# Retention attention and two expert layers on one core: zero-filled half chunks, first-expert weight splits in half-size pieces, and an earlier load of the second weight quad

## The chip, the cores and the metric

The kernel runs on one core of one Trainium2 chip, as a single launch. The metric is device time in microseconds (us); lower is better. Five engines work side by side: TensorE (PE in the profile, with its weight loads as PEld), VectorE (DVE), ScalarE (ACT), GpSimd (POOL), and SyncE (SP), which here issues most of the DMA transfers.

## What is computed

The reference, cut to what matters (8 batches, 8 heads, 576 tokens per batch, head size 64; 4608 tokens of width 512; 8 experts):

```python
scores = scale * np.matmul(q, k.transpose(0, 1, 3, 2))
Dmat = np.where(rel >= 0, gamma[:, None, None] ** rel[None, :, :], 0.0)
ret = np.matmul(scores * Dmat[None], v)            # attention with decay, no softmax
x = ret as 4608 rows of 512
expert_idx = argmax(x @ w_gate);  gate_w = softmax probability of that expert
out[mask] = gate_w[mask, None] * (np.maximum(x[mask] @ w1[e], 0.0) @ w2[e])   # for each expert e
h = out @ w_in;  g = h * np.cos(h);  result = g @ w_out
```

## The kernel before, in words

There are three stages, one behind the other, and TensorE carries all three.

**Attention** walks 40 steps, 8 batches of 5 chunks of tokens (`CH`: four of 128 and a last one of 64, the half chunk). The loop over `i` is a software pipeline written out by hand: iteration `i` turns the keys of chunk `i+1` (`transposes`, L307), forms the masked products of queries and keys of chunk `i` (`scores`, PE L323, DVE L327), scales the keys of chunk `i+2` (`decay_k`, DVE L298), and finishes chunk `i-1`: `inter` (PE L348) adds what the running state of earlier chunks gives into the PSUM tile `xps`, `intra` (PE L358) adds the chunk's own part, DVE L361 takes `xps` away into `xt`, and PE L367 updates the state. `rows` (PE L379) turns chunk `i-2` back into rows and gate logits; ACT L381 and DVE L382 take them from PSUM. `xps` has one buffer, so the next `inter` waits until DVE L361 has read the last one. Each engine runs its instructions in the order of the program.

For the half chunk the order differs: its `inter` is called first thing in the iteration, ahead of `transposes`, and a small ACT copy named `between` (L554) reads `xps` so that `intra` starts behind it. The half chunk's `intra` multiplies over 64 rows.

Weights are used as a high and a low part in a reduced fp32 format: an ACT cast makes the high part, and a DVE subtraction the low one. For expert 0 this is done inside the attention loop by `unit_split` (ACT L202, DVE L203): eight splits of 128 x 1024, one every fourth iteration from `i` = 9 to 37. The DVE subtraction stands between `decay_k` and the `xt` multiplication of the same iteration. `unit_load` brings the weights in on SP's queue.

**The experts** (`layer1` L722, `layer2` L737) follow, 24 steps of work per expert. In the last expert `layer2` runs its four column blocks at steps 20 to 23; ACT L739 copies each result from PSUM into `yev`, of which there are two buffers, and SP L741 stores it into `ydT`. At step 16 `ws_load(0)` (L867) brings the first weight quad of the last stage into one of two `wquad` buffers. They lie where the last expert's first-layer weights were.

**The last stage** takes 72 quads. `product` (L1143) of quad `i` needs `units[2, i]`, that is `ws_load(i)`, and the operands `near` and `far` made by `enter` (ACT L642, DVE L643); `gate` and `down` (L1218) follow. Before the stage there is a branch for rare cases (`tc.If(late > 0)`, L1112) that is not taken here. SP gets past it only when its transfers have landed. Then come eight small matmuls into a spare PSUM bank (`warm(NWARM3)`, L212), the load of the token numbers (L1224), `ws_load(1)`, the three `far` operands, and the loop.

Of the kernel before, what the change touches and what calls it, by code (L numbers as in the profile page):

```python
# [22 lines left out]
P = 128  # L23
H = 8
# [17 lines left out]
NWARM3 = 8  # L42
# [76 lines left out]
def attn_moe_kernel(ctx, tc, qt, kv, wg, w1, w2, win, wout, ctab, out):  # L119
# [77 lines left out]
    def unit_split(key, g, pool):  # L197
        s = staged.pop((key, g))
        if g == 0:
            units[key] = pool.tile([P, 2, 4, 512], F32R, tag=unit_tag(pool, key), name="wunit")  # L200
        u = units[key]
        nc.scalar.copy(out=u[:, 0, 2 * g:2 * g + 2], in_=s)  # L202
        nc.vector.tensor_sub(out=u[:, 1, 2 * g:2 * g + 2], in0=s, in1=u[:, 0, 2 * g:2 * g + 2])  # L203

# [10 lines left out]
    with ExitStack() as actx:  # L215
# [53 lines left out]

        steps = [(b, c) for b in range(B) for c in range(NCH)]  # L270
# [10 lines left out]
        def load_kv(i):  # L281
            b, c = steps[i]
            o, n = CH[c]
            t = ap3.tile([P, 2, H, D], F32, tag="ldkv", name="ldkv", bufs=6)
            nc.sync.dma_start(out=t[:n].rearrange("p s h d -> p s (h d)"), in_=kv[b * SEQ + o:b * SEQ + o + n])
            st[i]["k"], st[i]["v"] = t[:, 0], t[:, 1]
# [26 lines left out]
        def scores(i):  # L313
            b, c = steps[i]
            o, n = CH[c]
            s = st[i]
            pT = ap2.tile([P, H, P], F32, tag="pT", name="pT")
            scs = [ps1.tile([P, 4, P], F32, tag="sc", name="sc", bufs=3) for g in range(2)]

            for j in range(4):  # L320
                for g, r in ((0, 0), (1, D), (0, D), (1, 0)):
                    if r < n:
                        mm(out=scs[g][r:r + D, j, :n], lhsT=s["kpT"][D * g:D * g + D, j, r:r + D],  # L323
                           rhs=s["qT"][D * g:D * g + D, j, :n], start=(j == 0), stop=True, skip_group_check=True)
            m = mask[:n, :n].unsqueeze(1).to_broadcast([n, 4, n])
            for g in range(2):
                nc.vector.tensor_mul(out=pT[:n, g::2, :n], in0=scs[g][:n, :, :n], in1=m)  # L327
            s["pT"] = pT
# [22 lines left out]
        def intra(i):  # L351
# [4 lines left out]
            for h in range(H):  # L356
                k, r = place_of(h)
                mm(out=xp[r:r + D, k, :n], lhsT=s["v"][:n, h, :], rhs=s["pT"][:n, h, :n],  # L358
# [187 lines left out]
        wq = [(key, g) for key in w_units(0) for g in range(2)]  # L546
        waiting = []
        between = ap1.tile([P, 2, 2, 1], F32, name="between")
        for i in range(NS + 5):

            short = 1 <= i <= NS and CH[steps[i - 1][1]][1] <= D
            if short:
                inter(i - 1)
                nc.scalar.copy(out=between, in_=st[i - 1]["xp"].rearrange("p (a j) t -> p j a t", a=2)[:, 0:2, :, 0:1])  # L554
            if i + 1 < NS:
                transposes(i + 1)
            if i < NS:
                scores(i)
            if i + 2 < NS:
                decay_k(i + 2)  # L560
            if i >= 9 and (i - 9) % 4 == 0 and (i - 9) // 4 < len(wq):
                unit_split(*wq[(i - 9) // 4], upA)
            if i == 0:
                setup()
            if 1 <= i <= NS:
                if not short:
                    inter(i - 1)
# [8 lines left out]
            if 0 <= i - 2 < NS:  # L576
                rows(i - 2)
            to_spread, placed[:] = placed[:], []
# [11 lines left out]
            if i >= 6 and (i - 6) % 4 == 0 and (i - 6) // 4 < len(wq):  # L590
                unit_load(ap3, *wq[(i - 6) // 4])

        assert not tabled and not routed and not waiting and not placed
        assert not tabled and not routed
# [65 lines left out]
    with ExitStack() as mctx:  # L660
# [285 lines left out]
        for e in range(E):  # L946
# [9 lines left out]
            for i, (hf, l, k) in enumerate(work):  # L956
# [38 lines left out]
                if e + 1 == E and i == 16:  # L995
                    ws_load(0)
# [122 lines left out]
    warm(NWARM3, psA.tile([P, 512], F32, tag="h", name="hps", bufs=4), ident)  # L1119


# [110 lines left out]
    ws_load(1)  # L1232
# [81 lines left out]
```

## Time and profile before

| | us |
|---|---|
| median of 3 runs | 1423.28 (1420.9 to 1426.21) |
| the profiled execution | 1419.5 |
| its span in the profile | 1417.7 |
| PE busy | 1381.1 (97% of the span) |
| DVE busy | 964.5 (68%) |
| ACT busy | 705.6 (50%) |
| POOL busy | 223.0 (16%) |

The span is one execution from the first to the last instruction that the profiler saw; the execution's own time is 1.8 us longer. A busy share is an average over the three stages. The rows further down show single stretches: for each group, what the engine did, for how long, and in square brackets how long it had been idle before and on what it had waited.

### The profile page before, as it was taken

Reading aid. Unit: us, or ns where it says so; the run is one execution under the profiler, and the core shown is the slowest. Engines: PE = TensorE matmul, PEld = TensorE weight load, DVE = VectorE, ACT = ScalarE, POOL = GpSimd, SP = SyncE. Lnnn points to the kernel's source line nnn. Section 1 sums busy time; section 2 is a strip of 40 time slices with the busy share of each in tenths; the row PEclk is TensorE's granted clock in tenths of the full one; section 3 lists DMA queues with packets and bytes.
Section 4 is the critical chain, followed back from the end, with each engine's and each line's share of the span. In section 5 each row is a group of like instructions: output and inputs, shape, how many; then the busy total and the mean of one; then the engine's idle time right before and its main releaser. Section 6 shows DMA issues by size and latency. Waiting matters only on the chain.

```text
span 1417.7 us, 28604 instructions
## 1 busy us (share of the span) xinstructions
PE 1381.1 (97%) x11427; PEld 1284.0 (91%) x11427; DVE 964.5 (68%) x1953; ACT 705.6 (50%) x1405; POOL 223.0 (16%) x334
## 2 busy tenths in 40 slices
PE   8999979999999999998999999999999999999998
PEld 6888859999999999997999999899999999999997
DVE  5878768675888676854667666676667667676654
ACT  2444414444554544533556555565555655555554
POOL 3444441223221323200000010100101010010101
PEclk9999979999999999999999999999999999999999
DMA  7777725566776766795464564645646455555541
GB/s 240 231 243 232 234 73 173 183 220 211 242 251 201 224 206 229 251 384 203 178 230 172 191 232 162 249 169 197 226 157 241 182 213 196 196 199 197 187 175 64
DMA packets 81306, 292.23 MB, mean 206 GB/s; under 512 B 13476, under 2 KB 22128, under 8 KB 70928
## 3 DMA queue, kind: packets, MB, share of 16 engines
q1 hardware_dynamic: 68240, 248.33, 50.9%
q0 software_dynamic: 12928, 42.02, 8.6%
q8 instruction: 91, 1.49, 0.4%
q14 instruction: 47, 0.39, 0.1%
HBM read 238.85 MB, written 51.47 MB: 205 GB/s over the span
## 4 chain that ended last, share of the span: by engine, by line
PE 42%; issue 11%; POOL 1%; DMA 1%; ACT 0%; POOLq 0%
PE acc L1218 22%; PE hps L1143 20%; POOL out_dram L1200 1%; DMA wquad<-ws 1%; PE hps L212 0%; POOLq L1310 0%; POOL spare L156 0%; ACT ka L1173 0%; ACT orow L1198 0%; ACT gh L1184 0%; PE acc L1229 0%; POOLq L1200 0%
## 5 line engine op out<-in xcount | busy, mean ns | idle before, releaser
L1218 PE MATMUL acc<-wunit,gh 128*128 128x512 f32 x1152 | 358.3, 392 | 0.1
L1143 PEld LDWEIGHTS hps<-far,wquad 128*128 128x128 f32 x1920 | 244.6, 191 | 7.3
L1143 PE MATMUL hps<-far,wquad 128*128 128x256 f32 x1920 | 249.3, 283 | 0.0
L1218 PEld LDWEIGHTS acc<-wunit,gh 128*128 128x128 f32 x1152 | 207.3, 189 | 36.2 <-ACT gh L1184 0.3
L1218 PE MATMUL acc<-wunit,gl 128*128 128x512 f32 x576 | 224.4, 390 | 0.0
L722 PE MATMUL hps<-xT,wunit 128*128 128x256 f32 (+6 forms) x1536 | 208.6, 296 | 0.9 <-ACT xT L707 0.7
L737 PE MATMUL hps<-hh,wunit 128*128 128x256 f32 (+6 forms) x1024 | 207.7, 298 | 0.0
L722 PEld LDWEIGHTS hps<-xT,wunit 128*128 128x128 f32 x1536 | 206.4, 188 | 1.4 <-ACT xT L707 0.9
L737 PEld LDWEIGHTS hps<-hh,wunit 128*128 128x128 f32 x1024 | 164.3, 188 | 0.1
L1200 POOL DMA_INDIRECT out_dram<-orow,perm x36 | 35.0, 972 | 757.2 <-DVE orow L1196 751.4
L1143 PE MATMUL hps<-near,wquad 128*128 128x256 f32 x1104 | 147.5, 286 | 4.4 <-DMA wquad<-ws 4.4
L737 PE MATMUL hps<-hl,wunit 128*128 128x256 f32 (+6 forms) x512 | 151.3, 296 | 0.0
L1143 PEld LDWEIGHTS hps<-near,wquad 128*128 128x128 f32 x1104 | 142.9, 194 | 8.2 <-issue 4.6
L1218 PEld LDWEIGHTS acc<-wunit,gl 128*128 128x128 f32 x576 | 108.2, 188 | 24.7 <-DVE gl L1186 1.1
L1180 DVE SCALAR_TENSOR_TENSOR sa<-sa,quad 128x512 f32<-128x512 f32 x144 | 99.1, 688 | 42.8 <-ACT sa L1178 42.8
L1184 ACT CAST gh<-sa 128x512 fp32r<-128x512 f32 x144 | 89.6, 622 | 74.8 <-DVE sa L1180 74.8
L1154 DVE TENSOR_TENSOR part<-hps,part 128x256 f32<-128x256 f32 x72 | 30.6, 425 | 132.1 <-PE hps L1143 126.7
L1186 DVE TENSOR_TENSOR gl<-sa,gh 128x512 fp32r<-128x512 f32 x144 | 98.9, 687 | 20.4 <-ACT gh L1184 14.9
L1175 DVE SCALAR_TENSOR_TENSOR sa<-quad,ka 128x512 f32<-128x512 f32 x144 | 99.0, 687 | 12.2 <-ACT ka L1173 12.2
L1153 ACT COPY part<-hps 128x256 f32<-128x256 f32 x72 | 26.8, 372 | 144.2 <-PE hps L1143 137.9
L737 PEld LDWEIGHTS hps<-hl,wunit 128*128 128x128 f32 x512 | 96.5, 188 | 0.0
L1177 ACT ACTIVATE sa<-sa 128x512 f32<-128x512 f32 x144 | 91.3, 634 | 8.8 <-DVE sa L1175 8.8
(195 smaller groups left out, 1897.1 us busy)
## 6 DMA issues: line engine op xcount, KB each, us to landing
wquad<-ws SPq DMA_DIRECT2D x72, 1792.0 KB, 7.4
wst<-in_moe_w_dram SPq DMA_DIRECT2D x64, 512.0 KB, 5.1
ldkv<-in_kv_dram SPq DMA_DIRECT2D x32, 512.0 KB, 4.7
ws<-cvo POOLq DMA_DIRECT2D x56, 256.0 KB, 3.8
ldq<-in_qt_dram SPq DMA_DIRECT2D x32, 256.0 KB, 4.3
xd<-xs SPq DMA_DIRECT2D x32, 256.0 KB, 2.5
cvw<-in_moe_w_in_dram SPq DMA_DIRECT2D x16, 512.0 KB, 4.8
cvw<-in_moe_w_out_dram SPq DMA_DIRECT2D x16, 512.0 KB
```

Source lines behind the costliest of these rows:

```text
L722: mm(out=ph[:, :n], lhsT=u[:, a, kc, f0:f0 + P], rhs=t[:, bq, kc, :n], start=(idx == 0), stop=(idx == 11))
L737: mm(out=py[:, :n], lhsT=u[:, w], rhs=t[:, :n], start=(fc == 0 and g == 0), stop=(fc == 7 and g == 2))
L1143: mm(out=o, lhsT=u[:, s, kc, a], rhs=x[:, bq, kc], start=(s in (0, 1, 2) and idx == 0), stop=(idx == 5), skip_group_check=True)
L1153: nc.scalar.copy(out=p1, in_=x[:, :HT])
L1154: nc.vector.tensor_add(out=u2, in0=y[:, :HT], in1=p1)
L1175: nc.vector.scalar_tensor_tensor(out=sa, in0=x, scalar=INV2PI, in1=ka, op0=ALU.mult, op1=ALU.subtract)
L1177: nc.scalar.activation(out=sa, in_=sa, func=AF.Sin, scale=math.pi)
L1180: nc.vector.scalar_tensor_tensor(out=sa, in0=sa, scalar=-1.0, in1=x, op0=ALU.add, op1=ALU.mult)
L1184: nc.scalar.copy(out=gh, in_=sa)
L1186: nc.vector.tensor_sub(out=gl, in0=sa, in1=gh)
L1200: ins = nc.gpsimd.indirect_dma_start(out=out[:, :], out_offset=bass.IndirectOffsetOnAxis(ap=perm[:, k:k + 1], axis=0), in_=o, in_offset=None)
L1218: mm(out=acc2[T][c], lhsT=pair[n][:, fh, c % 2 * P:(c % 2 + 1) * P], rhs=u[:, w, fc % 4], start=(q == 0 and fh == 0 and n == 0 and w == 0) ...
```

## The change

- The half chunk's `inter` goes back to its usual place behind `scores`, and the copy `between` is gone. The half chunk has tiles of its own: `halfkv` (two, by the batch's parity) and `halfpT` (one). Rows 64 to 127 of the value half and of `halfpT` are zeroed once by POOL, and `intra` multiplies over all 128 rows.
- Expert 0's weights are split in 16 pieces of 128 x 512 in place of 8 of 128 x 1024: one piece in each batch's fifth iteration and two in the next one, from `i` = 9 to 34. The ACT casts stand behind `transposes`, the DVE subtractions behind `rows`. The loads move to iterations 6, 7, 11, 15, 16, 21, 25 and 26.
- `ws_load(1)` is issued at step 20 of the last expert in place of behind the branch.
- The eight matmuls of `NWARM3` are gone.

```diff
+        halfkv = [ap1.tile([P, 2, H, D], F32, name=f"halfkv{i}") for i in range(2)]
+        halfpT = ap1.tile([P, H, D], F32, name="halfpT")
+        for t in [t.rearrange("p s h d -> p s (h d)")[D:, 1] for t in halfkv] + [halfpT[D:]]:
+            nc.gpsimd.memset(t, 0.0)
...
-            t = ap3.tile([P, 2, H, D], F32, tag="ldkv", name="ldkv", bufs=6)
+            t = ap3.tile([P, 2, H, D], F32, tag="ldkv", name="ldkv", bufs=6) if n == P else halfkv[b % 2]
...
-            pT = ap2.tile([P, H, P], F32, tag="pT", name="pT")
+            pT = ap2.tile([P, H, P], F32, tag="pT", name="pT") if n == P else halfpT
...
-                mm(out=xp[r:r + D, k, :n], lhsT=s["v"][:n, h, :], rhs=s["pT"][:n, h, :n],
+                mm(out=xp[r:r + D, k, :n], lhsT=s["v"][:, h, :], rhs=s["pT"][:, h, :n],
...
-        wq = [(key, g) for key in w_units(0) for g in range(2)]
+        wq = dict(zip((6, 7, 11, 15, 16, 21, 25, 26), [(key, g) for key in w_units(0) for g in range(2)]))
+        pieces = [(key, f) for key in w_units(0) for f in range(4)]
...
-            short = 1 <= i <= NS and CH[steps[i - 1][1]][1] <= D
-            if short:
-                inter(i - 1)
-                nc.scalar.copy(out=between, in_=st[i - 1]["xp"].rearrange("p (a j) t -> p j a t", a=2)[:, 0:2, :, 0:1])
             if i + 1 < NS:
                 transposes(i + 1)
+            now = [pieces.pop(0) for _ in range({NCH - 1: 1, 0: 2}.get(i % NCH, 0) if i > NCH else 0) if pieces]
+            for key, f in now:
+                if f == 0:
+                    units[key] = upA.tile([P, 2, 4, 512], F32R, tag="unit", name="wunit")
+                nc.scalar.copy(out=units[key][:, 0, f], in_=staged[key, f // 2][:, f % 2])
             if i < NS:
                 scores(i)
             if i + 2 < NS:
                 decay_k(i + 2)
-            if i >= 9 and (i - 9) % 4 == 0 and (i - 9) // 4 < len(wq):
-                unit_split(*wq[(i - 9) // 4], upA)
...
-                if not short:
-                    inter(i - 1)
+                inter(i - 1)
                 intra(i - 1)
...
                 rows(i - 2)
+            for key, f in now:
+                nc.vector.tensor_sub(out=units[key][:, 1, f], in0=staged[key, f // 2][:, f % 2], in1=units[key][:, 0, f])
...
-            if i >= 6 and (i - 6) % 4 == 0 and (i - 6) // 4 < len(wq):
-                unit_load(ap3, *wq[(i - 6) // 4])
+            if i in wq:
+                unit_load(ap3, *wq[i])
...
-                if e + 1 == E and i == 16:
-                    ws_load(0)
+                if e + 1 == E and i in (16, 20):
+                    ws_load((i - 16) // 4)
...
-    warm(NWARM3, psA.tile([P, 512], F32, tag="h", name="hps", bufs=4), ident)
...
-    ws_load(1)
```

How the order of instructions changes. First VectorE in iterations 9 and 10, the end of the second batch (`pT` are the masks, `kp` the scaled keys, `xt` the multiplication that frees `xps`, `lgt` the logits), before:

```order
L327 TENSOR_TENSOR pT<-sc,ca 64x4x64 x2
L298 TENSOR_TENSOR kp<-ldkv,ca 128x512
L203 TENSOR_TENSOR wunit<-wst,wunit 128x1024
L361 TENSOR_TENSOR xt_126<-xps,gx 128x512
L382 TENSOR_REDUCE lgt_132<-rw 128x8 x2
L327 TENSOR_TENSOR pT<-sc,ca 128x4x128 x2
L298 TENSOR_TENSOR kp<-ldkv,ca 128x512
L361 TENSOR_TENSOR xt_122<-xps,gx 128x4x64
```

and with the change:

```order
L323 TENSOR_TENSOR halfpT<-sc,ca 64x4x64 x2
L294 TENSOR_TENSOR kp<-ldkv,ca 128x512
L357 TENSOR_TENSOR xt_126<-xps,gx 128x512
L378 TENSOR_REDUCE lgt_132<-rw 128x8 x2
L572 TENSOR_TENSOR wunit<-wst,wunit 128x512
L323 TENSOR_TENSOR pT<-sc,ca 128x4x128 x2
L294 TENSOR_TENSOR kp<-ldkv,ca 128x512
L357 TENSOR_TENSOR xt_122<-xps,gx 128x4x64
L502 TENSOR_TENSOR tab<-tab,lg 128x120
L378 TENSOR_REDUCE lgt_132<-rw 128x8 x2
L572 TENSOR_TENSOR wunit<-wst,wunit 128x512 x2
```

The subtraction has moved from ahead of `xt` to behind the logits, and has become three smaller ones over the two iterations.

TensorE at the end of a batch, where a half chunk is finished, before:

```order
L379 MATMUL rw<-wgi,xt_124 128x136 x4
L348 MATMUL xps<-ldq,sbd_128 64x64 x8
L307 MATMUL tp<-ct,kp 128x128 x4
L323 MATMUL sc<-ldq,kpT 64x128 x16
L358 MATMUL xps<-pT,ldkv 64x64 x8
```

and with the change:

```order
L375 MATMUL rw<-wgi,xt_124 128x136 x4
L303 MATMUL tp<-ct,kp 128x128 x4
L319 MATMUL sc<-ldq,kpT 64x128 x16
L344 MATMUL xps<-ldq,sbd_128 64x64 x8
L354 MATMUL xps<-halfpT,halfkv_135 64x64 x8
```

`inter`, which writes `xps`, now has `transposes` and `scores` ahead of it.

SyncE at the end of the last expert, before (`ydT` are the stores of the four column blocks):

```order
L867 DMA wquad<-ws_74 128x3584
L1008 REGISTER_ALU
L1008 DMA idc<-sidT 5x128
L741 ISA
L741 DMA ydT<-yev 128x232
L741 ISA
L741 DMA ydT<-yev 128x232
```

and with the change:

```order
L861 DMA wquad<-ws_74 128x3584
L1002 REGISTER_ALU
L1002 DMA idc<-sidT 5x128
L735 ISA
L735 DMA ydT<-yev 128x232
L861 DMA wquad<-ws_74 128x3584
L735 ISA
L735 DMA ydT<-yev 128x232
```

The second quad's load now stands between the first and the second of the four stores.

## Rows read from the trace of the kernel before

**Rows 1.** Stretches: busy us (instructions) per engine, PEclk granted clock, DMA share, GB/s.

```profile
0.00:216.00 216.00, 192.78 (x3455) 169.49 (x3456) 155.27 (x455) 75.91 (x180) 88.49 (x140) 0.95 0.65 207
...
643.50:666.00 22.50, 17.09 (x109) 15.59 (x109) 10.21 (x20) 8.73 (x17) 0.00 (x0) 0.85 0.68 249
```

**Rows 2.** Timeline, DVE in iteration 9: start, us, what.

```profile
50.46 1.21 DVE L203 TENSOR_TENSOR wunit<-wst,wunit 128x1024 fp32r<-128x1024 f32 x1
51.60 0.67 DVE L361 TENSOR_TENSOR xt<-xps,gx 128x512 f32<-128x512 f32 x1
```

**Rows 3.** Timeline, PE at two batch ends, the first with a split, the second without.

```profile
52.41 0.46 PE L348 MATMUL xps<-ldq,sbd 64*64 64x64 f32 x16 [0.97 <-DVE lgt L382]
...
96.01 0.63 PE L367 MATMUL S<-ldkv,kp 128*64 128x64 f32 x16
...
97.70 0.46 PE L348 MATMUL xps<-ldq,sbd 64*64 64x64 f32 x16
...
99.60 0.64 PE L358 MATMUL xps<-pT,ldkv 64*64 64x64 f32 x16
```

**Rows 4.** Timeline, PE: the same place in four batches, five iterations apart each.

```profile
30.15 0.66 PE L307 MATMUL tp<-ct,kp 128*128 128x128 f32 x4
...
121.08 0.66 PE L307 MATMUL tp<-ct,kp 128*128 128x128 f32 x4
...
144.81 0.65 PE L307 MATMUL tp<-ct,kp 128*128 128x128 f32 x4
...
167.67 0.66 PE L307 MATMUL tp<-ct,kp 128*128 128x128 f32 x4
```

**Rows 5.** Half-size subtractions in the expert stage: count, min/median/max ns, first to last start.

```profile
L854 DVE TENSOR_TENSOR wunit<-wst,wunit x112: 673/686/744, 223.7 to 602.2; 128x512 fp32r<-128x512 f32 x112
```

**Rows 6.** Timeline, POOL at the start.

```profile
10.26 1.78 POOL L253 TENSOR_SCALAR gx<-gx,ca 128x128 f32<-128x128 f32 x3 [7.73 <-DMA ca<-in_consts_dram]
```

**Rows 7.** Timeline, PE from the last expert into the last stage.

```profile
643.29 0.27 PE L737 MATMUL hps<-hl,wunit 128*128 128x232 f32 x1
644.15 0.60 PE L212 MATMUL hps<-ct 128*128 128x256 bf16 x4 [0.59 <-ACTq L1112]
...
645.51 3.12 PE L1143 MATMUL hps<-near,wquad 128*128 128x256 f32 x24
648.47 2.31 PE L1143 MATMUL hps<-far,wquad 128*128 128x256 f32 x18
655.19 5.21 PE L1143 MATMUL hps<-near,wquad 128*128 128x256 f32 x24 [4.42 <-DMA wquad<-ws]
```

**Rows 8.** Timeline, ACT over the same stretch.

```profile
641.24 0.35 ACT L739 COPY yev<-hps 128x232 f32<-128x232 f32 x1 [2.61 <-DMA ydT<-yev]
643.64 0.35 ACT L739 COPY yev<-hps 128x232 f32<-128x232 f32 x1 [2.05 <-PE hps L737]
646.38 0.62 ACT L642 CAST far<-yfirst 128x512 fp32r<-128x512 f32 x1 [2.39 <-SPq L1112]
```

**Rows 9.** Timeline, SP's queue: the first quad's load, the second of four stores.

```profile
627.56 0.32 SPq L867 DMA_DIRECT2D wquad<-ws  x1
...
638.66 0.33 SPq L741 DMA_DIRECT2D ydT<-yev  x1
```

**Rows 10.** The chain that ended last, at the second quad: start, us, what.

```profile
647.22 7.83 DMA wquad<-ws
655.19 7.36 PE hps L1143 x42
```

**Rows 11.** DMA issues of one line: count, KB each, median us from issue to landing.

```profile
wquad<-ws SPq DMA_DIRECT2D x72, 1792.0 KB, 7.4
```

**Rows 12.** Stretches, columns as in rows 1: three in which TensorE stood.

```profile
6.50:9.00 2.50, 0.02 (x1) 0.05 (x1) 0.69 (x1) 0.59 (x1) 0.00 (x0) 1.00 1.01 350
650.80:653.00 2.20, 0.00 (x0) 0.00 (x0) 1.88 (x5) 0.63 (x1) 0.00 (x0) 1.00 1.05 440
653.00:655.20 2.20, 0.01 (x1) 0.04 (x1) 0.00 (x0) 0.00 (x0) 0.00 (x0) 0.53 0.91 358
```

More of the change, by code (lines that the diff above doesn't have):

```diff
@@ L41 @@
 NWARM2 = 11
-NWARM3 = 8
 INV2PI = 1.0 / (2.0 * math.pi)
@@ L195, in unit_load @@
         staged[key, g] = s
[L197 to L203, printed above, removed]
     def w_units(e):
@@ L545, in attn_moe_kernel @@
         decay_k(1)
-        wq = [(key, g) for key in w_units(0) for g in range(2)]
+        wq = dict(zip((6, 7, 11, 15, 16, 21, 25, 26), [(key, g) for key in w_units(0) for g in range(2)]))
+        pieces = [(key, f) for key in w_units(0) for f in range(4)]
         waiting = []
-        between = ap1.tile([P, 2, 2, 1], F32, name="between")
         for i in range(NS + 5):
-            short = 1 <= i <= NS and CH[steps[i - 1][1]][1] <= D
-            if short:
-                inter(i - 1)
-                nc.scalar.copy(out=between, in_=st[i - 1]["xp"].rearrange("p (a j) t -> p j a t", a=2)[:, 0:2, :, 0:1])
             if i + 1 < NS:
                 transposes(i + 1)
+            now = [pieces.pop(0) for _ in range({NCH - 1: 1, 0: 2}.get(i % NCH, 0) if i > NCH else 0) if pieces]
[3 more added lines that the diff above has]
+                nc.scalar.copy(out=units[key][:, 0, f], in_=staged[key, f // 2][:, f % 2])
             if i < NS:
@@ L589, in attn_moe_kernel @@
                 loads(i + 4)
-            if i >= 6 and (i - 6) % 4 == 0 and (i - 6) // 4 < len(wq):
-                unit_load(ap3, *wq[(i - 6) // 4])
-        assert not tabled and not routed and not waiting and not placed
-        assert not tabled and not routed
+            if i in wq:
+                unit_load(ap3, *wq[i])
+        assert not tabled and not routed and not waiting and not placed and not pieces
         rp = ps1.tile([P, 8, P], F32, tag="x", name="xps").rearrange("p a t -> p (a t)")
```

## The prediction, made before the changed kernel was run

> **What bounds the kernel now.** I first read busy time by stretch, to see where TensorE is not the limit, then the timeline and the waits inside those stretches. In the attention stage TensorE is busy 192.78 of 216 us; in the 22.5 us around the start of the last stage it is busy 17.09, and its clock is granted at 0.85 on average [rows 1]. Everywhere else it hardly stands, so the change can only pay in these two stretches, both of which it touches.
>
> In attention the thing to see is a queue on VectorE. In iteration 9 the subtraction of the weight split (1.21 us from 50.46) stands ahead of the `xt` multiplication, which starts at 51.60 [rows 2]. TensorE's early `inter` writes the single-buffered `xps` and needs `xt` done: it stands 0.97 us and starts at 52.41. The wait is labelled with the logits, the next instruction on VectorE. At a batch end without a split the same `inter` starts at 97.70 with no wait [rows 3]. So the early place of `inter` costs nothing alone; with a split it does.
>
> Is that one case or all? Batches differ in how many splits they hold. From 30.15 to 121.08 there are four batches with one split each (iterations 9, 13, 17, 21), 90.93 us; the batch from 144.81 to 167.67, 22.86 us, has one (33); the one from 121.08 to 144.81, 23.73 us, has two (25, 29) [rows 4]. One-split batches average (90.93 + 22.86) / 5 = 22.76 us, so a second split costs 23.73 - 22.76 = **0.97 us**, the wait seen directly. I charge it to all eight, wherever they stand: 8 x 0.97 = 7.8 us.
>
> At the handover the experts end at 643.56 (643.29 + 0.27). The warm-up matmuls begin at 644.15, and the first quad's products run from 645.51 to 650.78 (648.47 + 2.31). Then TensorE stands 4.42 us for the second quad's weights [rows 7]. Their load was issued at 647.22 and took 7.83 us; the products behind it took 7.36 us, against 650.78 - 645.51 = 5.27 us for the first quad [rows 10]. That is the clock: it was granted whole until 653.00, in a stand that began at 650.78, and averaged 0.53 from there to 655.20 [rows 12], about the lower level (1.2 of 2.4 GHz).
>
> **The change, part by part.** *Splits.* Removed: eight waits, 7.8 us. Added: 16 subtractions of 0.686 us [rows 5], 11.0 us of VectorE against 8 x 1.21 = 9.7 us, so 1.3 us more work, but behind the logits. The next work there is the masks, which need the next `scores`. From `inter` to `intra` at the clean batch end, with `transposes` and `scores` between, TensorE takes 99.60 - 97.70 = 1.9 us [rows 3]; the largest group of pieces is 2 x 0.686 = 1.37 us, so it fits. If that cover fails, the masks come late and then `rows`, whose PSUM buffers the masks free. Bounds: nothing, or a wait in proportion to a piece's length, 0.97 x 0.686 / 1.21 = 0.55 us, 16 times, 8.8 us. I take 0.05 us each, 0.8 us, near the lower end, since the pieces stand behind the work that TensorE waits for. The casts stand behind the key copy and delay only ACT copies that wait for matmuls two microseconds later. Loads come at least two iterations ahead of their first piece. Net gain in attention: 7.8 - 0.8 = **7.0 us**.
>
> *Half chunk.* `inter` moves behind two groups of matmuls, and `xt` has that time more. The copy `between` goes. The 64-row `intra` takes 0.64 us for 16 passes; a 128-row group of equal count and width (the state update) takes 0.63 us [rows 3]. So the zeros cost no TensorE time: 0. POOL's three fills fall into the 7.73 us in which it stands for its constants [rows 6]: 0; without that cover they delay decay tables that are needed only in iteration 2 and later.
>
> *Second quad.* Its load moves from 647.22 to just behind the first of the last four stores, at about 636.4 (the second store is issued at 638.66 [rows 9]). It needs 7.4 to 7.8 us [rows 10, 11], so it lands near 644, six microseconds ahead of its use. Gone: the 4.42 us wait, and with it 7.36 - 5.27 = 2.1 us of slow clock.
>
> But the load is queued ahead of three stores, and they free `yev`. A store behind a large load waits: the copy at 641.24 had stood 2.61 us for the first store, which had the first quad's load of 627.56 ahead of it in the queue; the next copy, at 643.64, waited only for TensorE [rows 8, 9]. If the second store lands with the load ahead of it, at about 644.0, the fourth `yev` copy, which needs that buffer, starts there in place of 643.64 and ends at 644.4. The Trainium skill, page DMA: Bandwidth & Descriptors, section Queues, rings and completion order, says that on each DMA engine the descriptors of one ring are consumed in ring order; by that rule the store cannot pass the load, and the trace's late copy agrees. My two ends for this: no delay, and the fourth copy late by the 2.61 us that the third one stood, at 646.25. I take 0.4 us, since the load's landing is the nearer row.
>
> *No warm-up.* TensorE was released at 644.15, 0.16 us behind the end of the last copy (643.64 + 0.35) [rows 7, 8]. With the copy ending at 644.4 the first quad starts at 644.5, not 645.51: 1.0 us gained. Its `far` operands come when SP is past the branch, which was 2.39 us behind the copy's end [rows 8]: 646.8, and 0.62 us of cast and a subtraction of about 0.69 us [rows 5] make the first one whole at 648.1. The first 24 matmuls take 648.47 - 645.51 = 2.96 us, to 647.5, so I put 0.4 us of new wait there. Gain left: 0.6 us. The stand grows from 0.59 us to about 1.0 us. At 6.50 to 9.00 TensorE stood as good as all of 2.50 us and the clock stayed at 1.00; at 653 it fell after some 2.3 us of standing [rows 12]. So I expect it to hold. The Trainium skill, page TensorE: Matmul & The Clock Gate, section Why this matters for your kernels, speaks against this edit: it warns of idle gaps between bursts of matmuls, which put the array back on its lower clock. By that rule the first quad would be slow; rows 12 show both outcomes.
>
> *Third quad.* Its load still starts when the first quad's products end, now about 650.2. Its use comes one product and one half `down` later: 5.27 + 2.9, at 658.4; 7.4 us [rows 11] land it at 657.9. Half a microsecond of slack is thin, and the gate chain of the first quad no longer hides behind a slow product: I charge 0.5 us for both.
>
> Handover: 4.4 + 2.1 + 0.6 - 0.5 = **6.6 us**.
>
> **Sum.** 7.0 + 6.6 = 13.6 us off the profiled execution's 1419.5 (span 1417.7 and 1.8 around it): 1405.9. That execution lies 3.8 us under the median of the runs, 1423.28; on the median's scale the forecast is 1423.3 - 13.6 = **1409.7 us**. The experts and the steady last stage run at TensorE's pace and only shift.
>
> **The rivals.**
> 1. *The pieces still show.* VectorE, busy 155 of 216 us in attention [rows 1], falls behind at batch ends and half of the old wait stays. For: three subtractions in two neighbouring iterations, with the routing behind them. Against: their place. Attention gives 3.5 in place of 7.0: 1413.2.
> 2. *The clock falls at the handover.* With the warm-up gone and the stores late, TensorE's stand becomes one like that from 650.78. The first quad is slow by 2.1 us, and starts up to 646.25 - 644.0 = 2.2 us later: 1409.7 + 4.3 = 1414.0.
> 3. *The wait moves to the third quad.* Its load finds two loads of encoded rows, 512 KB each, ahead of it in SP's queue: 1,048,576 bytes at the 440 GB/s of a full stretch [rows 12] are 2.4 us, so it lands at 650.2 + 7.4 + 2.4 = 660.0, 1.6 us late, and if the clock falls, 2.1 us more: 1411.3 to 1413.4.
> 4. *Slower than before.* Small pieces cost as much each as a whole split did, because what counts is a late instruction on VectorE and not its length: 16 x 0.97 = 15.5 in place of 7.8, 7.7 us lost, more than the handover's 6.6: 1424.4. It decides from (7.8 + 6.6) / 16 = 0.90 us for each piece. Against: the pieces come behind `xt`, not ahead of it.
> 5. *The early load does nothing*, because SP, held by stores that wait for `yev`, issues it late. SP issues it ahead of the second store, whose issue is seen at 638.66 [rows 9], so it would have to slip nine microseconds: 1409.7 + 6.5 = 1416.2.
>
> **How the numbers follow.** Forecast 0.60; rivals in order 0.13, 0.12, 0.10, 0.02, 0.03. A difference of 0.5% is 7.1 us, about what a measurement of this kernel can tell from no change, so the edge is 1416.2. The forecast and the first three rivals lie beyond it, 0.95, unless two of the rivals meet, for which I take 0.07; with rival 5's 0.03 that is the same: faster 0.88, same 0.10, slower 0.02. The low end is no cost for pieces, gate chain and stores (0.8 + 0.5 + 0.4 + 0.4 = 2.1 us less) and 2.4 us for the spread of the runs (1420.9 against the median): 1405. The high end takes in two of the first three rivals together: 1417.
>
> **What would show it.** Right: no TensorE wait at batch ends; batches of about 21.8 us (22.76 - 0.97); no wait for `wquad` at the second quad; a clock at 1.00 from 644 to 666; third quad's products near 658 less what attention gained. Wrong: a wait on masks or logits in iterations 10, 15, 20; a clock under 1.00 in the first quad's products; a `yev` copy that waits for its store until past 645 (on the old time axis); a wait for the third quad.

## The result, and the profile after

The changed kernel took **1408.1 us** (median of 4 runs, 1405.9 to 1411.57). The kernel before, on the same chip, took 1422.09 us (median of 4, 1418.86 to 1426.21). The ratio is **0.9915, interval 0.9895 to 0.9934**: faster by 0.85%, 12.1 us (the two medians lie 14.0 us apart; the ratio with its interval is what is used here). The forecast of 13.6 us off is a ratio of 0.9904, inside the interval; 1409.7 us stood against 1408.1. The sum was right, but by luck: attention gave more than its term, the handover less, and the two errors cancelled.

To see that, cut both profiled executions at five marks that every kernel here has: the first `transposes` of iteration 5 (30.15 in [rows 4]), the last `transposes` of attention, the first matmul of expert 0, the end of the experts, and the first product of the third quad. The numbers are taken on TensorE's timeline: each mark is the start of its instruction, the end of the experts is the end of their last matmul, and "rest" ends with the span.

| stretch, us | before | after | difference |
|---|---|---|---|
| start, to iteration 5 | 30.15 | 33.13 | +2.98 |
| attention, steady | 150.32 | 142.27 | -8.05 |
| last iterations, to expert 0 | 33.83 | 32.52 | -1.31 |
| experts | 429.26 | 431.30 | +2.04 |
| handover, to the third quad | 21.99 | 18.91 | -3.08 |
| rest | 752.15 | 751.67 | -0.48 |
| span | 1417.70 | 1409.80 | -7.90 |

The first mark has one flaw. Where the half chunk's `inter` comes early, its 0.39 us lie ahead of the mark (29.76 to 30.15 before); in the other kernels it lies behind. With equal work on both sides, the start differs by 3.37 us and steady attention by -8.44.

The difference of this pair of executions, 7.9 us, is smaller than that of the medians, and the two rows with a plus say why. This execution (1411.57 us) is the longest of the four, and its slow stretches are clock. Stretches of the changed kernel; columns as in [rows 1]:

```profile
8.00:10.00 2.00, 0.57 (x4) 0.58 (x4) 0.69 (x1) 0.00 (x0) 0.00 (x0) 0.90 1.04 338
10.00:12.00 2.00, 2.00 (x34) 1.59 (x32) 0.00 (x0) 0.58 (x1) 1.18 (x2) 0.50 1.02 391
...
18.00:20.00 2.00, 2.00 (x30) 1.93 (x27) 1.92 (x4) 0.00 (x0) 2.00 (x4) 0.54 0.09 33
...
212.00:214.00 2.00, 2.00 (x11) 2.00 (x11) 0.37 (x3) 0.26 (x1) 0.00 (x0) 0.50 0.64 194
```

The granted clock is 0.50, the lower of its two levels, from 10 to past 18 us and again in the first six microseconds of expert 0. At 6.50 to 9.00 before it was 1.00 in the same place [rows 12]. That is no part of the change: in the ten kernels that follow, the start took from 29.32 to 34.16 us, 29.80 and 29.82 with all of the changed attention stage, and the experts 428.25 to 429.48. So these two rows are left out of the account, and what the change did is read from the other four: -8.05, -1.31, -3.08 and -0.48, together **-12.9 us** (-13.3 with the 0.39), near the 12.1 of the runs.

**Attention.** VectorE's timeline around a batch end with a piece, then TensorE's over the same microseconds:

```profile
53.14 0.69 DVE L294 TENSOR_TENSOR kp<-ldkv,ca 128x512 f32<-128x512 f32 x1 [0.27 <-DMA ldkv<-in_kv_dram]
53.75 0.68 DVE L357 TENSOR_TENSOR xt<-xps,gx 128x512 f32<-128x512 f32 x1
54.35 0.17 DVE L378 TENSOR_REDUCE lgt<-rw 128x8 f32<-128x16 f32 x1
54.81 0.17 DVE L378 TENSOR_REDUCE lgt<-rw 128x8 f32<-128x16 f32 x1 [0.29 <-ACT xs L377]
54.91 1.01 DVE L572 TENSOR_TENSOR wunit<-wst,wunit 128x512 fp32r<-128x512 f32 x1
55.90 1.29 DVE L323 TENSOR_TENSOR pT<-sc,ca 128x512 f32<-128x512 f32 x2
```

```profile
54.21 0.60 PE L303 MATMUL tp<-ct,kp 128*128 128x128 f32 x4
54.74 1.10 PE L319 MATMUL sc<-ldq,kpT 64*64 64x128 f32 x32
55.66 0.41 PE L344 MATMUL xps<-ldq,sbd 64*64 64x64 f32 x16
56.01 0.68 PE L354 MATMUL xps<-halfpT,halfkv 128*64 128x64 f32 x16
```

The order of [rows 2] is turned round: `xt` comes first, then the logits, then the piece. The masks start right behind it, at 55.90, and no matmul waits. The 16 pieces, as in [rows 5] (count, min/median/max ns, first to last start):

```profile
L572 DVE TENSOR_TENSOR wunit<-wst,wunit x16: 679/683/1006, 54.9 to 163.0; 128x512 fp32r<-128x512 f32 x16
```

The one shown is the longest; the median is the 0.69 us that was assumed. `inter` (0.41 us) and `transposes` (0.60) are also a little shorter than the 0.46 and 0.66 of [rows 3, 4].

The place of [rows 4], of which the line at 54.21 above is one, four and five batches later:

```profile
140.65 0.60 PE L303 MATMUL tp<-ct,kp 128*128 128x128 f32 x4
162.26 0.60 PE L303 MATMUL tp<-ct,kp 128*128 128x128 f32 x4
```

The four batches from 54.21 to 140.65 take 21.61 us each, and so does the one behind them, with three pieces in each. The forecast said "about 21.8".

**Handover.** TensorE, then ACT, then SP's queue, as [rows 7 to 9]:

```profile
638.95 0.27 PE L731 MATMUL hps<-hl,wunit 128*128 128x232 f32 x1
642.08 5.49 PE L1134 MATMUL hps<-near,wquad 128*128 128x256 f32 x24 [2.86 <-ACTq L1106]
647.42 2.62 PE L1134 MATMUL hps<-far,wquad 128*128 128x256 f32 x18
649.88 3.04 PE L1134 MATMUL hps<-near,wquad 128*128 128x256 f32 x24
652.76 2.32 PE L1134 MATMUL hps<-far,wquad 128*128 128x256 f32 x18
```

```profile
636.62 0.35 ACT L733 COPY yev<-hps 128x232 f32<-128x232 f32 x1 [2.33 <-PE hps L731]
641.54 0.35 ACT L733 COPY yev<-hps 128x232 f32<-128x232 f32 x1 [4.56 <-DMA ydT<-yev]
645.44 0.62 ACT L636 CAST far<-yfirst 128x512 fp32r<-128x512 f32 x1 [3.55 <-SPq L1106]
```

```profile
631.64 0.35 SPq L735 DMA_DIRECT2D ydT<-yev  x1
632.10 0.36 SPq L861 DMA_DIRECT2D wquad<-ws  x1
634.32 7.93 SPq L735 DMA_DIRECT2D ydT<-yev  x3
```

The wait for `wquad` of [rows 7] is gone: the second quad starts at 649.88 behind the first without a gap. But the fourth `yev` copy, which would have come 2.68 us behind the third (2.33 + 0.35), at 639.30, starts at 641.54: it waits for a store issued at 634.32 behind the load of 632.10, and that store lands at 641.44. TensorE has nothing to do until that copy is out and stands 2.86 us. Then the first 24 products take 5.49 us in place of about 3. The clock over that stretch:

```profile
640.00:642.00 2.00, 0.00 (x0) 0.00 (x0) 0.00 (x0) 0.35 (x1) 0.00 (x0) 0.77 0.14 47
642.00:644.00 2.00, 1.92 (x9) 1.92 (x10) 0.00 (x0) 0.00 (x0) 0.00 (x0) 0.50 0.25 76
...
648.00:650.00 2.00, 2.00 (x20) 2.00 (x18) 1.07 (x3) 0.37 (x1) 0.00 (x0) 1.00 0.99 365
```

So the wait for the second quad was taken away, and a wait for the last copy and a slow first quad were put in place of the greater part of it.

### The profile page after: what moved, and what is told of

Its sections match the earlier page's. It is cut to its first block, busy times and chain, and to the rows that moved or that the text cites. A ratio compares the mean times of both kernels' runs of the same rounds, so it can differ in the third digit from the quotient of the medians.

```text
span 1409.8 us, 28606 instructions
## 1 busy us (share of the span) xinstructions
PE 1383.1 (98%) x11419; PEld 1288.0 (91%) x11419; DVE 965.0 (68%) x1961; ACT 704.8 (50%) x1405; POOL 220.5 (16%) x337
## 4 chain that ended last, share of the span: by engine, by line
PE 49%; issue 5%; POOL 0%; POOLq 0%; ACT 0%
PE acc L1209 25%; PE hps L1134 24%; POOL out_dram L1191 0%; POOLq L1300 0%; ACT orow L1189 0%; ACT gh L1175 0%; POOL spare L155 0%; PE acc L1220 0%; POOLq L1191 0%
## 5 line engine op out<-in xcount | busy, mean ns | idle before, releaser
L716 PE MATMUL hps<-xT,wunit 128*128 128x256 f32 (+6 forms) x1536 | 211.5, 299 | 0.7 <-ACT xT L701 0.7
L716 PEld LDWEIGHTS hps<-xT,wunit 128*128 128x128 f32 x1536 | 209.3, 191 | 1.4 <-ACT xT L701 1.1
L1166 DVE SCALAR_TENSOR_TENSOR sa<-quad,ka 128x512 f32<-128x512 f32 x144 | 98.8, 686 | 12.3 <-ACT ka L1164 12.3
```

The source lines that it names most:

```text
L716: mm(out=ph[:, :n], lhsT=u[:, a, kc, f0:f0 + P], rhs=t[:, bq, kc, :n], start=(idx == 0), stop=(idx == 11))
L1166: nc.vector.scalar_tensor_tensor(out=sa, in0=x, scalar=INV2PI, in1=ka, op0=ALU.mult, op1=ALU.subtract)
```

## The experiments

Each kernel was timed over five rounds against the kernel before on the same chip; "handover" is the stretch of the table above. The questions were which part brought what, and then what holds the handover.

### One half of the change at a time

*Attention only* undoes the handover part (base: the changed kernel):

```
-                if e + 1 == E and i in (16, 20):
-                    ws_load((i - 16) // 4)
+                if e + 1 == E and i == 16:
+                    ws_load(0)
...
+    warm(NWARM3, psA.tile([P, 512], F32, tag="h", name="hps", bufs=4), ident)
...
+    ws_load(1)
```

> The attention part of the change alone; the handover is that of before (second quad loaded behind the branch, eight warm-up matmuls). My theory: in the changed kernel's trace batches last 21.61 us against 22.42 to 23.73 before, so the steady part of attention gains about 8 us, and the handover keeps its wait of 4 to 4.5 us for the second quad and its slow clock: 8 us faster than before, 1414 if before is 1422, ratio 0.9945. Rival, that the attention gain is mostly given back in the tail and the first expert, where the clock is granted later in the changed kernel's trace: 4 us faster or less, ratio 0.997.

*Handover only* keeps those three edits and has all of attention as before.

> The handover part alone (second quad's load at step 20 of the last expert, no warm-up matmuls); attention is that of before. My theory: the third copy into yev is on time, the fourth one waits 4 to 5 us for the store that stands behind the second quad's load, TensorE stands 2.5 to 3 us ahead of the first quad, there is no wait for the second quad: 3 to 6 us faster than before, ratio 0.996 to 0.998, depending on whether the clock falls in the stand. Rival, that the load itself is the whole story and the store plays no part: 6.6 us or more, ratio 0.995, and no stand over 1 us.

Measured: attention only 1411.74 us, ratio 0.9933 (0.992 to 0.9945), 9.5 us off. Handover only 1417.65 us, ratio 0.998 (0.9968 to 0.9992), 2.8 us off. The two make 12.3 us; the whole change made 12.1. So the parts add up, and the handover brought less than half of the 6.6 us it had been given. Attention alone gave a little more than the 8 us expected of it, and handover alone about the lower end of its 3 to 6. The traces agree: steady attention 142.27 with the attention part, 149.98 without; handover 23.18 without the handover part, 18.83 with it. TensorE at the handover of the second kernel:

```profile
647.23 4.62 PE L1141 MATMUL hps<-near,wquad 128*128 128x256 f32 x24 [3.30 <-ACTq L1111]
652.25 2.42 PE L1141 MATMUL hps<-far,wquad 128*128 128x256 f32 x18 [0.41 <-ACT part L1151]
```

The same stand and the same slow first quad stand here with the old attention stage, so they belong to the handover edits.

### Pieces and half-chunk order apart

*Pieces only* is the kernel before with the pieces and their loads, the early `inter` kept:

```
-        wq = [(key, g) for key in w_units(0) for g in range(2)]
+        wq = dict(zip((6, 7, 11, 15, 16, 21, 25, 26), [(key, g) for key in w_units(0) for g in range(2)]))
+        pieces = [(key, f) for key in w_units(0) for f in range(4)]
...
-            if i >= 9 and (i - 9) % 4 == 0 and (i - 9) // 4 < len(wq):
-                unit_split(*wq[(i - 9) // 4], upA)
```

> The kernel before with the half-size pieces and their load schedule alone; the half chunk's early inter, its 64-row intra and the ACT copy stay, the handover is that of before. My theory (the prediction's): the early inter costs nothing without a split ahead of xt, so batches last 21.7 to 21.8 us and nearly the whole attention gain is here: 7 to 8 us, ratio 0.9945 to 0.995. Rival, that the early inter is what hurts and the pieces only help with it gone: batches of 22.3 us or more, a gain of 3 us or less, ratio 0.998.

*Order only* is the kernel before with the padded half chunks in the usual order and the eight whole splits kept:

```
-            if short:
-                inter(i - 1)
-                nc.scalar.copy(out=between, in_=st[i - 1]["xp"].rearrange("p (a j) t -> p j a t", a=2)[:, 0:2, :, 0:1])
...
-                if not short:
-                    inter(i - 1)
+                inter(i - 1)
```

> The kernel before with the half chunk's usual order, zeroed rows and own tiles alone; the eight whole splits stay where they were, the handover is that of before. My theory: only the waits of the early inter go (three of the eight splits hit it, about 1 us each) and 0.15 us in each batch; the waits of scores on late logits stay: 3 to 4 us, ratio 0.997 to 0.998. Rival, that the order is the cause: 7 us or more, ratio 0.995.

Measured: pieces only 1414.39 us, 0.9957 (0.9942 to 0.9972), 6.1 us off, below the 7 to 8 expected; steady attention 144.26, that is 6.06 less than before. Order only 1419.36 us, 0.9998 (0.9983 to 1.0013), no difference that the runs can tell, where 3 to 4 us had been expected; steady attention 148.71, 1.61 less (2.00 with the 0.39 us of the mark). With the pieces already in, the order is worth 144.26 - 142.27 = 1.99 us, or 2.38 with the 0.39. Two readings show where that comes from. In steady attention of pieces only, TensorE has two waits left that the changed kernel does not have: 0.50 us at 35.16, for an ACT copy, and 0.94 us at 97.15. Here is the second one, below VectorE's line in front of it:

```profile
95.70 0.70 DVE L298 TENSOR_TENSOR kp<-ldkv,ca 128x512 f32<-128x512 f32 x1 [1.02 <-DMA ldkv<-in_kv_dram]
...
97.15 0.46 PE L348 MATMUL xps<-ldq,sbd 64*64 64x64 f32 x16 [0.94 <-DVE lgt L382]
```

No split stands there. A load of keys came 1.02 us late, `xt` behind it came late too, and the early `inter` felt all of it. In the changed kernel `xt` has the time of `transposes` and `scores` as slack: at 53.14 the same key decay also waited for its load, 0.27 us, and no matmul noticed. In order only, the split is still ahead of `xt`, and TensorE now waits one place later:

```profile
49.58 1.21 DVE L203 TENSOR_TENSOR wunit<-wst,wunit 128x1024 fp32r<-128x1024 f32 x1
...
51.52 0.99 PE L328 MATMUL sc<-ldq,kpT 64*64 64x128 f32 x27 [0.17 <-DVE lgt L387]
```

Its waits of `scores` sum to 2.6 us in six places. So the early place did cost something alone: 0.94 us once, 0.50 us once, and some 0.16 us in each full batch (21.77 against 21.61).

The order also bears on the -1.31 of the last iterations (order only -1.10, pieces only -0.76). The `rw` products behind the last half chunk take 2.18 us in the three kernels with the early `inter` (before, handover only, pieces only), and 1.19 in the changed kernel and in order only. That is the clock, which falls one iteration later there; that the shorter waits ahead of it are the cause is argued, not shown. The size of this term is not firm either: with all of the changed attention stage the last iterations took from 31.23 to 32.52 us, from one kernel's execution to another's.

### What holds the handover

The first idea was the warm-up: put its eight matmuls back into the changed kernel.

```
+NWARM3 = 8
...
+    warm(NWARM3, psA.tile([P, 512], F32, tag="h", name="hps", bufs=4), ident)
```

> The changed kernel with the eight warm-up matmuls ahead of the first quad kept. My theory: they wait for the same ACT release as the first quad's products, so they start when the stand is over and cannot fill it; they take 1.3 us of TensorE (part of which covers the wait for the far operands) and the clock is low for them as it was for the products: 0 to 1.3 us slower than the changed kernel. Rival, that their removal is what lets the clock fall: clock whole in the first quad's products and 1 to 2 us faster than the changed kernel.

Measured: 1410.42 us, 0.9929 (0.9912 to 0.9945); handover 19.07, as without. TensorE:

```profile
636.27 1.87 PE L204 MATMUL hps<-ct 128*128 128x256 bf16 x8 [3.27 <-ACTq L1107]
637.79 3.79 PE L1137 MATMUL hps<-near,wquad 128*128 128x256 f32 x24
```

The warm-up waits for the same copy as the quad, so it comes when the clock has already fallen. It shortens the first 24 products from 5.49 to 3.79 us and takes 1.52 itself. Its removal cost nothing and gave nothing that the runs can tell.

Next, the load's place in the queue. One kernel issues the second quad's load from ScalarE's DMA queue, in the same step; the other issues it one step later, behind the second store:

```
-        def ws_load(n):
+        def ws_load(n, eng=None):
...
-                    ws_load((i - 16) // 4)
+                    ws_load((i - 16) // 4, nc.scalar if i == 20 else None)
```

> The changed kernel with the second quad's load issued by ScalarE's DMA queue at the same step, so that it is not ahead of the stores in SyncE's queue. Theory of queue order: the stores pass it, the fourth yev copy starts within 1 us of the end of its matmuls, TensorE's stand ahead of the first quad shrinks from 2.86 us to about 1 us and the time falls by 2 to 4 us against the changed kernel (ratio to before 0.988 to 0.990). Rival, shared bandwidth (the engines move the load and the stores share what is left): the copy still waits 2 us or more and the time stays within 1 us of the changed kernel's.

```
-                if e + 1 == E and i in (16, 20):
-                    ws_load((i - 16) // 4)
+                if e + 1 == E and i in (16, 21):
+                    ws_load((i - 16) // 5)
```

> The changed kernel with the second quad's load one step later, at step 21, behind the second store. The store that frees the fourth copy's buffer is then ahead of the load. Theory of queue order: the fourth copy does not wait, the first quad starts 2 us earlier relative to the end of the experts (stand about 0.6 to 1 us), but the third and fourth stores stand behind the load, SyncE passes the branch no earlier than now, and the far operands come late: a wait of 1 to 2 us between the first 24 and the other 18 matmuls of the first quad. Net 1 to 3 us faster than the changed kernel, ratio to before 0.989 to 0.991. Rival, shared bandwidth: the fourth copy still waits 2 us or more and nothing is gained.

Measured: ScalarE's queue 1408.35 us, 0.9915 (0.9901 to 0.993), handover 18.63; one step later 1407.14 us, 0.9912 (0.9897 to 0.9926), handover 19.98. Neither moved the time. ACT in the first:

```profile
634.18 0.35 ACT L733 COPY yev<-hps 128x232 f32<-128x232 f32 x1 [6.62 <-DMA ydT<-yev]
```

With the load out of SP's ring the late copy is the third, and later still, 6.62 us: its store, issued at 624.90 beside a load issued at 624.54, finds engines that are full (share 0.90 to 1.07) from 618 to 632 us. The DMA queues from 629 to 631 us (packets, MB, share; q1 is SP's, and q10 moves data only in this kernel, where ScalarE issues the load):

```profile
q10 hardware_dynamic: 48, 0.69, 92.7%
q1 hardware_dynamic: 46, 0.04, 5.9%
```

Up to 628.5 us SP's queue was still moving the first quad's load, ahead of the store. From then on the store got its turns: the two queues moved about as many packets, but one of the store is 928 bytes and one of the load 14,336. So the order behind one load is not the whole of it; here the theory of queue order failed, and the rival, shared bandwidth, held. In the second, every copy was on time, as the theory of queue order had it, but TensorE stood for another reason:

```profile
633.68 0.63 PE L1134 MATMUL hps<-near,wquad 128*128 128x256 f32 x3 [0.62 <-ACTq L1106]
637.69 4.64 PE L1134 MATMUL hps<-near,wquad 128*128 128x256 f32 x21 [3.38 <-issue]
```

Three products, then 3.38 us in which the profile shows nothing that it waited for. The load is under way in that gap. The DMA queues from 635 to 636 us:

```profile
q8 instruction: 1, 0.02, 6.1%
q14 instruction: 2, 0.02, 4.3%
```

From 633 to 635 no packet of an instruction queue moved, and 94% of the engines' time went to data. That TensorE stood for instructions that came late is argued from this, not shown. The load landed at 637.50, 0.19 us ahead of the product that went on, and the trace does not tell the two apart.

So the third idea: what hurts is not one load's place but that large transfers are under way at all when the experts end. *Deferral* moves four loads of 1,024 KB, needed by later quads only, out of the last expert:

```
-                elif i % 2 == 0 and i < 16:
-                    wide_unit((0, 2, 1, 3)[i // 4], i // 2 % 2, nc.sync)
+                elif i % 2 == 0 and i < 8:
+                    wide_unit((0, 2)[i // 4], i // 2 % 2, nc.sync)
...
             ws_load(i + 2)
+        if i < 4:
+            wide_unit((1, 3)[i // 2], i % 2, nc.sync)
```

> The changed kernel with four of the eight last-layer weight loads of the last expert (1 MB each, steps 8 to 14; first used by the fifth quad) issued behind the quad loads of the last stage's first four turns instead. It takes 4 MB out of the DMA queue ahead of the handover. Theory of the backlog (the stand at the handover comes from DMA work that is still in the queue when the experts end: it delays the store that frees the copy's buffer, and TensorE's own instruction fetch): the first quad's load lands about 9 us earlier, the second one before the experts end, the fourth copy waits under 1 us, TensorE's stand ahead of the first quad is 0.6 to 1 us and the clock stays whole: 3 to 5 us faster than the changed kernel, ratio to before 0.988 to 0.989. Rival, that the order of load and store in the queue alone counts: the copy still waits 2 us or more and the time is that of the changed kernel, 0.9915.

Measured: 1406.67 us, 0.99 (0.9882 to 0.9918); handover 17.17. TensorE, and the fourth copy:

```profile
636.85 0.62 PE L1134 MATMUL hps<-near,wquad 128*128 128x256 f32 x3 [1.29 <-ACTq L1106]
638.38 3.81 PE L1134 MATMUL hps<-near,wquad 128*128 128x256 f32 x21 [0.90 <-issue]
```

```profile
636.34 0.35 ACT L733 COPY yev<-hps 128x232 f32<-128x232 f32 x1 [3.02 <-DMA ydT<-yev]
```

Stand and copy's wait are shorter, and nothing waits for the deferred loads later (rest 751.66). But neither theory held as it stood: the copy still waited 3.02 us, the clock fell (0.50 from 640 to 642), and the time is no different from the changed kernel's that the runs can tell. The second quad's load, issued at 628.43, still has the second store behind it. The buffer that it fills is free once the last matmul of the experts' first layer is out, at 624.85 here (623.79 + 1.06). That gives the kernel that decides, *deferral and step 19*:

```
-                if e + 1 == E and i in (16, 20):
-                    ws_load((i - 16) // 4)
+                if e + 1 == E and i in (16, 19):
+                    ws_load((i - 16) // 3)
```

> The changed kernel with the four 1024-KB loads of later quads moved behind the third to sixth quad load (as in the run that only did this), and the second quad's load issued one step earlier, at step 19, ahead of all four last stores. In the trace with the deferral alone the DMA engines moved nothing from 616 to 620 us, the second layer of matmuls that frees the buffer ended at 624.9, and the fourth copy still waited 3.02 for a store that stood behind the load. Theory A (the handover is late only because a large transfer is under way there: stores and instruction packets stand behind it): the load is issued near 625, lands by 630, no copy waits for a store at the end (0 in place of 3.02), PE stands under 1.3 before the first quad, the clock stays 1.00, and from the experts' end to the third quad it takes 14 to 15.5 us in place of 17.2 with the deferral alone and 18.9 in the changed kernel; time 3 to 5 us below the changed kernel, 1403 to 1405 against 1420 of before. Theory B (the stand and the slow clock come from the branch and its instruction fetch alone, whatever is transferred): no copy waits, but PE still stands 2.5 to 3.5 and the clock falls to 0.50; 17 to 19 us, 1406 to 1408.

and beside it step 19 without the deferral:

> The changed kernel with the second quad's load at step 19 alone; the four 1024-KB loads stay ahead of it. Theory A (transfers under way decide): the queue holds some 10 us of those loads when this one is issued near 625 (the DMA share of the changed kernel is 0.86 to 1.07 in every window from 600 to 638 us), so it lands at 633 to 636, the first store stands behind it, the third copy waits 4 to 7 us as in the run with the load on ScalarE's queue, the clock falls, 18 to 19.5 us from the experts' end to the third quad, and the time is that of the changed kernel within 2 us. Theory C (only the order of load and stores in SP's queue decides, and a load ahead of all stores is harmless): no copy waits, the clock stays 1.00, 14 to 15.5 us, and the time is 3 to 5 us below the changed kernel.

Measured: deferral and step 19 **1403.42 us, 0.9891 (0.987 to 0.9912)**, handover 16.17; step 19 alone 1408.11 us, 0.9918 (0.9899 to 0.9938), handover 18.70. With the deferral, TensorE, ACT and the clock:

```profile
632.96 0.62 PE L1134 MATMUL hps<-near,wquad 128*128 128x256 f32 x3 [0.59 <-ACTq L1106]
634.09 2.66 PE L1134 MATMUL hps<-near,wquad 128*128 128x256 f32 x21 [0.51 <-issue]
638.02 2.42 PE L1134 MATMUL hps<-far,wquad 128*128 128x256 f32 x18 [1.27 <-ACT part L1144]
```

```profile
630.92 0.35 ACT L733 COPY yev<-hps 128x232 f32<-128x232 f32 x1 [3.48 <-DMA ydT<-yev]
632.45 0.35 ACT L733 COPY yev<-hps 128x232 f32<-128x232 f32 x1 [1.17 <-PE hps L731]
636.04 0.62 ACT L636 CAST far<-yfirst 128x512 fp32r<-128x512 f32 x1 [3.24 <-SPq L1106]
```

```profile
630.00:632.00 2.00, 2.00 (x21) 2.00 (x20) 0.00 (x0) 0.35 (x1) 0.00 (x0) 1.00 0.06 16
632.00:634.00 2.00, 0.99 (x7) 0.71 (x6) 0.00 (x0) 0.35 (x1) 0.00 (x0) 1.00 0.35 115
634.00:636.00 2.00, 1.91 (x17) 1.90 (x17) 0.00 (x0) 0.00 (x0) 0.00 (x0) 1.00 0.08 20
```

The DMA engines are quiet (0.06) when the experts end, the fourth copy waits only for TensorE, and the clock stays at 1.00. Theory A held for both kernels in the main. Without the deferral the same load sits in the backlog, and the copies wait longer than ever:

```profile
636.22 0.73 ACT L733 COPY yev<-hps 128x232 f32<-128x232 f32 x2 [6.29 <-DMA ydT<-yev]
```

It missed in two points. No copy was to wait for a store, but the third one stood 3.48 us for the first store, which follows the load in SP's queue; it came about 1.15 us late, while TensorE still had the fourth block to multiply. And the handover took 16.17 us where 14 to 15.5 had been expected, because the `far` casts start only at 636.04, 3.24 us behind the end of the last copy, and TensorE waits 1.27 us for the copy `part`, which stands behind them on ACT.

This version is the fastest that was run, 4.7 us under step 19 alone in the medians of the same chip. Its interval against the kernel before overlaps that of the changed kernel, and the two were not timed side by side; what the traces show, in one execution of each, is the handover, 16.17 against 18.91 us.

## Why the prediction was right, point by point

- **The splits**: 7.0 us forecast. Pieces only gained 6.06 in steady attention and would have gained 7.00 without the one wait that a late key load caused (0.94). The charge of 0.97 per split and the small cost of a piece were right, and so was the reason: place in VectorE's queue, not length.
- **The half-chunk order**: forecast 0, since "the early place of `inter` costs nothing alone". Measured 1.99 us with the pieces in (2.38 with the 0.39 of the mark), and a part of the 1.31 in the last iterations. The step failed because one clean batch end [rows 3] was read as the rule: there the wait was zero, but so was the slack, and any late `xt` went straight to TensorE. The zeros did cost nothing: 0.68 us for the 16 padded passes.
- **The early load**: the 4.42 us wait and the slow second quad went, as forecast. The third quad was not late, and its half microsecond charge was not needed: from the second quad's `far` products to the third quad it took 652.76 to 658.13 = 5.37 us, before 660.24 to 665.55 = 5.31.
- **The fourth copy**: "I take 0.4 us, since the load's landing is the nearer row." Measured 641.54 - 639.30 = 2.24 us late. The upper end, 2.2 us, was the truth. Two steps failed. The load was to land 7.6 us behind its issue; its last packet in the trace ends at 640.68, 8.6 us behind, since the first quad's load still filled the queue ahead of it (DMA share 1.00 from 632 to 634). And the store was to land with the load; it landed at 641.44, 0.8 us later, while the third store's packets were moving too. The trace has a landing for one of the four stores only, this second one:

```profile
ydT<-yev SPq DMA_DIRECT2D x4, 116.0 KB, 7.1
```

- **The clock**: "So I expect it to hold." With a stand of about 1.0 us it might have; the stand was 2.86 us, and the clock fell in it (0.77 from 640 to 642), ahead of the first product. This followed from the copy. Of the eight kernels with the new handover, seven ran the first quad at 0.50 for a part; in the one whose stands were 0.59, 0.51 and 1.27 us the clock held. The Trainium skill, page TensorE: Matmul & The Clock Gate, section Why this matters for your kernels, warns of idle gaps between bursts. The trace agrees in direction, but not in size: a stand of 2.29 us (step 19 alone) and stands of 1.29 and 0.90 (deferral alone) were followed by 0.50, and these are shorter than the gaps that the page names. The stand of 1.0 us in the forecast is shorter too, so "by that rule the first quad would be slow" did not follow from the page.
- **The handover's sum**: 6.6 forecast, 3.08 in the trace, 2.8 by the runs of that half alone. This is rival 2, which had 4.3 us lost of the 6.6.
- **The total**: 13.6 forecast. Add 2.4 us that attention gave beyond its 7.0 (8.05 + 1.31 - 7.0), take off the 3.5 us that the handover fell short: 12.5, against 12.1 measured. The time was forecast well because two errors had opposite signs, and that was luck.

Of the other rivals: the pieces did not show (1), no wait moved to the third quad (3), small pieces did not cost as much as whole splits (4), and SP issued the load on time, at 632.10 (5).

## What to carry to other kernels

A load moved ahead of the place where it is waited for does not get its wait for nothing: look at what else uses the queue in that place, and follow each store behind it to the buffer that it frees and the engine that waits for that buffer. Empty the queue there first (what is needed last goes last), then move the load as early as its buffer allows. And a matmul that follows right behind its producer costs nothing in the clean trace but has no slack, so it pays for everything that comes late; put independent work between the two.

## What the runs showed of the hardware that was not expected

- A store of 116 KB waited for a backlog that was not only ahead of it in its own queue: with the load on ScalarE's queue the third copy still stood 6.62 us. The Trainium skill, page DMA: Bandwidth & Descriptors, section Queues, rings and completion order, says that each DMA engine takes its rings in turn. The trace agrees: 46 packets of SP's queue went beside 48 of ScalarE's in the 2 us shown above. With as many packets from each, the store of 928-byte packets went at the pace of the load of 14,336-byte ones. Both parts counted: of the time from the store's issue at 624.90 to the copy at 634.18, 3.6 us went by behind the first quad's load in SP's own queue, up to 628.5, and most of the rest in taking turns. Moving the load to another queue helped nothing.
- With a large load under way, TensorE stood 3.38 us behind its third matmul after the branch with no wait that the profile shows. In the kernel whose transfers were done by then, the same place took 0.51 us.
- A stand of 2.50 us at the start left the clock at 1.00 in the kernel before [rows 12], and a stand of 2.18 us in the changed kernel, up to 9.43, was followed by 0.50. How long TensorE stands does not alone tell what is granted next. The four executions of the changed kernel, from 1405.9 to 1411.57 us, had mean granted clocks from 0.992 down to 0.984; how much of their spread the clock makes is not shown.
